# Pair 14's loads ahead of the output weights, a score bank for one turn, and one exponential behind a tanh

## The chip, the cores and the metric

The kernel runs on one core of one Trainium2 chip. The metric is device time in microseconds (us), the median of a few executions. One further execution was recorded by the hardware profiler; all times within the program are from it, in us from the start of its span.

## What is computed

Attention over 8 batches of 12 heads (448 rows, head size 64), with a softmax over the keys, and then a gated feed-forward block on the 3584 rows of 768 numbers that it gives. The reference, cut to what matters:

```python
scores = scale * np.matmul(q, k.transpose(0, 1, 3, 2))
attn = np.exp(scores - np.max(scores, axis=-1, keepdims=True))
attn = attn / (np.sum(attn, axis=-1, keepdims=True) + 1e-09)
x = np.matmul(attn, v)          # then heads are laid side by side: 3584 x 768
g = x @ w_gate                  # 768 x 1536
silu = g * (1.0 / (1.0 + np.exp(-g)))
out = (silu * (x @ w_val)) @ w_out   # w_out is 1536 x 768
```

## The kernel before

Two heads make a pair, so there are 48 pairs, six to a batch. The work on a pair has these steps, with the lines that the profile shows for them:

- **Loads.** GpSimd's DMA queue brings q, k and v from HBM and turns fp32 into fp16 on the way (`load_qk16`, L157 and, for keys of pairs from 12 on, L138 in two halves; `load_v`, L168 and L138). The same queue brings the weights: gate and value in quarters of two DMAs each (L186), the output weights in two halves, wo0 and wo1, of one DMA of 128 x 12 x 384 numbers each (L188). Pairs below 6 are loaded ahead of everything, some pairs two at a time. Pairs 14 and 15 share one buffer and are loaded apart.
- **Turning q and k.** For pairs up to 10 TensorE turns them (`prep`, L258) into a PSUM tile that VectorE copies out (L259). From pair 11 on GpSimd copies q and k into one fp16 tile (L217 for pair 11, `prep_quad` with L194 from 12 on), and SP issues two DMA transposes for each pair (L220 and L224, or L196 and L200). The copies stand in the same GpSimd stream as the DMA issues.
- **Scores and exponentials.** TensorE multiplies q and k into one of three score banks (L299; from pair 12 on L268, and L281 for a block of rows that two pairs share: that of 12 and 13 needs the turned q and k of both). ScalarE takes the exponential of each bank (L307, L289).
- **Product with v.** Lines L325 and L333, L362 from pair 12 on. VectorE divides by the sums (L344 and L346, or L403 and L404), and the result is turned into X (L433 on TensorE with L440 on VectorE for pairs below 12, DMA transposes on SP after that).
- **Feed-forward block.** Groups of six matmuls with gate and value weights (L493), a tanh on ScalarE (L511), two steps on VectorE (L516 forms t from the tanh and the gate product, L519 multiplies it with the value product), and twelve matmuls with the output weights for each part of the output (L544), which ScalarE copies out (L551) and SP stores (L564). The first block takes all its products with wo0 ahead of those with wo1.

PSUM has three score banks, taken in turn by `stile`, and two smaller buffers (tag `f`), which products of v, value products, output products and, in some visits, a gate product share.

The order is written out by hand. After an opening list, a plan runs through visits of two or three score products each (two below pair 8, three from there); in each visit come the scores and exponentials, then turns, loads and copies for later pairs, then the products with v that are due, and a share of the feed-forward work. A dictionary `wq` says which loads are issued at the end of the visit in which a pair's first score product stands: `6: [("V", 3), ("o", 0)]` brings v of pairs 9 to 11 and wo0, `9: [("o", 1)]` brings wo1. From pair 14 on, q and k of a pair are asked for six pairs ahead, that of 14 in the visit in which pair 8 begins. The copies of pair 11 stand in that visit too, those of 12 and 13 in the visit of pair 9, of 14 in that of pair 10, of 15 in that of pair 11.

A DMA that GpSimd issues waits, by the semaphores that the program uses in a ring of eight, until the eighth DMA before it has landed. The stream is in order, so what stands behind such a wait stands still as well.

Of the kernel before, what the change touches and what calls it, by code (L numbers as in the profile page):

```python
# [12 lines left out]
AF = mybir.ActivationFunctionType  # L13
# [7 lines left out]
LA = 6  # L21
RB = 5
FIRST = 6
# [8 lines left out]
QUAD = 12  # L32
# [5 lines left out]
def kernel(  # L38
# [10 lines left out]
    nc = tc.nc  # L49
    B, H, S, D = q.shape  # L50
    DM = H * D
    DF = moe_w_gate.shape[1]
    P = 112
# [4 lines left out]
    NPAIR = B * NHP  # L58
    NGRP = NPAIR // GP
    GPB = NHP // GP  # L60
    sm_scale = float(D) ** -0.5
# [41 lines left out]
    def wslice(kind, fb, cb):  # L103
        i, off = divmod(fb * 128, DF // 4)
        return wgv[kind, i][:, cb, ds(off, 128)]
# [9 lines left out]
    def stile():  # L115
        sring.append(sring.pop(0))
        return sbanks[sring[-1]]

    def dummy(n, w=512):
        wp = ps_f.tile([128, 512], FP32, tag="f", name="wp")  # L120
        for _ in range(n):
            nc.tensor.matmul(wp[:, 0:w], lhsT=warm[:, 0:128], rhs=warm[:, 0:w], start=True, stop=True)
# [39 lines left out]
    def load_v(pr, n=1):  # L162
        b, h = divmod(2 * pr, H)
        if pr >= QUAD:
            vd = vraw[:, ds(pr % VS, n)].rearrange("p r h c d -> p (r h) (c d)")
            load_keys(nc.gpsimd, vd, v, 2 * pr, 2 * n)
            return
        nc.gpsimd.dma_start(  # L168
            vraw[0:P, ds(pr % VS, n)].rearrange("p r h c d -> p (r h) (c d)"),
            v[b, h : h + 2 * n].rearrange("h (p c) d -> p h (c d)", c=NC),  # L170
        )
# [18 lines left out]
    def prep_quad(pr):  # L190
        rq, rk = raw[pr]
        qk16 = attp.tile([128, 2, NC, 2, D], FP16, tag="qk16", name="qk16", bufs=3)
        for dst, src in ((qk16[:, 0], rk), (qk16[0:P, 1], rq)):
            nc.gpsimd.tensor_copy(dst.rearrange("p c h d -> p h c d"), src)  # L194
        qkT[pr] = attp.tile([128, NC * 128 + S], FP16, tag="qkT", name="qkT", bufs=QB)
        nc.sync.dma_start_transpose(  # L196
            qkT[pr][:, 0 : NC * 128].rearrange("p (c q) -> p c q", q=128),
            qk16[:, 0].rearrange("p c h d -> p (c h d)"),
        )
        nc.sync.dma_start_transpose(  # L200
            qkT[pr][:, NC * 128 :].rearrange("p (c q) -> p c q", q=P),
            qk16[0:P, 1].rearrange("p c h d -> p (c h d)"),
        )

    def prep(pr):
        if pr >= QUAD:
            return prep_quad(pr)
        rq, rk = raw[pr]
        if pr == 0 or pr >= NPE:
            qk16 = attp.tile([128, 2, NC, 2, D], FP16, tag="qk16", name="qk16", bufs=3)[0:P]  # L210
            for t, src in enumerate((rq, rk)):
                dst = qk16[:, 1 - t].rearrange("p c h d -> p h c d")
                if pr == 0:
                    nc.vector.tensor_copy(dst[:, 0], src[:, 0])
                    nc.scalar.activation(dst[:, 1], src[:, 1], AF.Copy)
                else:
                    nc.gpsimd.tensor_copy(dst, src)  # L217
        qkT[pr] = attp.tile([128, 2 * S + D], FP16, tag="qkT", name="qkT", bufs=QB)
        if pr >= NPE:
            nc.sync.dma_start_transpose(  # L220
                qkT[pr][:, 0 : 2 * S].rearrange("p (c q) -> p c q", q=P),
                qk16.rearrange("p t c h d -> p (t c h d)"),
            )
            nc.sync.dma_start_transpose(  # L224
                qkT[pr][:, 2 * S :].rearrange("p (c q) -> p c q", c=1),
                qk16[0:D, 1, 0].rearrange("p h d -> p (h d)"),
            )
            return None

        def turn0():  # L230
            for t in range(2):
                tp = stile()
                for c in range(NC):
                    for hx in range(2):
                        nc.tensor.matmul(
                            tp[ts(hx, 64), c // 2, ds(c % 2 * P, P)],
                            lhsT=qk16[:, 1 - t, c, hx],
                            rhs=ident[0:P, 0:P],
                            start=True,
                            stop=True,  # L240
                        )
                dst = qkT[pr][:, ts(1 - t, S)].rearrange("p (a x) -> p a x", a=2)
                nc.vector.tensor_copy(dst[:, 0], tp[:, 0, 0 : 2 * P])
                nc.scalar.activation(dst[:, 1], tp[:, 1, 0 : 2 * P], AF.Copy)
                if t == 0:
                    dummy(1, 256)
                    nc.vector.tensor_copy(qkT[pr][:, 2 * S :], tp[:, 0, 0:D])

        def turn():
            if pr < FIRST + 2:  # L250
                tp = stile()[:, 0].bitcast(FP16)
            else:
                tp = ps_f.tile([128, 1024], FP16, tag="f", name="tp")
            for i in range(2 * NC + 1):
                t, c = (1 - i // NC, i % NC) if i < 2 * NC else (0, 0)
                for hx in range(2):
                    src = raw[pr][t][:, hx, c, :]
                    nc.tensor.transpose(tp[ts(hx, 64), ts(i, P)], src, ident[0:P, 0:P])  # L258
            nc.vector.tensor_copy(qkT[pr][:], tp[:, 0 : 2 * S + D])  # L259

        return turn if pr else turn0
# [28 lines left out]
            e[:, 0 : 2 * S].rearrange("p (h q) -> p h q", h=2), s[:, :, 0:S], AF.Exp, scale=sm_scale  # L290
        )

    def qk(pr, c):
        if pr >= QUAD:
            return qk_quad(pr, c)
        t = qkT[pr]
        s = stile()
        for hx in range(2):
            nc.tensor.matmul(  # L299
                s[:, hx, 0:S],  # L300
                lhsT=t[ts(hx, 64), c * P : c * P + 128],
                rhs=t[ts(hx, 64), ds(S + (1 - hx) * D, S)],
                start=True,
                stop=True,
            )
        e = Es[pr % NE][:, ds(c * EB, 16)].rearrange("p (h b) x -> p h (b x)", h=2)
        nc.scalar.activation(e[:, :, 0:S], s[0:P, :, 0:S], AF.Exp, scale=sm_scale)  # L307

    def qk_half(pr, half, between=None):
        for c in (2 * half, 2 * half + 1):  # L310
# [177 lines left out]
    def ffn1_steps(kk, c0, n, hts, ahead):  # L488
        for fb in range(NFB):

            def group(kind, dst):
                for cb in range(NCB):
                    nc.tensor.matmul(  # L493
                        dst[:, 0:n],
                        lhsT=wslice(kind, fb, cb),
                        rhs=X[kk][:, cb, ds(c0, n)],
                        start=(cb == 0),
                        stop=(cb == NCB - 1),
                    )

            if fb < ahead:
                gp, vp = sbanks[begun[fb]][:, 0], sbanks[begun[fb]][:, 1]
            elif gate_small[0]:
                gate_small[0] = False
                gp = ps_f.tile([128, 512], FP32, tag="f", name="gp")
            else:
                gp = stile()[:, 0]
            if fb >= ahead:
                group("g", gp)
            sg = fp.tile([128, 512], FP32, tag="sg")  # L510
            nc.scalar.activation(sg[:, 0:n], gp[:, 0:n], AF.Tanh, scale=0.5)  # L511
            if fb >= ahead:
                vp = ps_f.tile([128, 512], FP32, tag="f", name="vp")
                group("v", vp)
            t1 = fp.tile([128, 512], FP32, tag="t1")
            nc.vector.scalar_tensor_tensor(  # L516
                t1[:, 0:n], sg[:, 0:n], 1.0, gp[:, 0:n], ALU.add, ALU.mult
            )
            nc.vector.scalar_tensor_tensor(  # L519
                hts[:, fb, 0:n], t1[:, 0:n], 0.5 * HS, vp[:, 0:n], ALU.mult, ALU.mult  # L520
            )
            if fb < ahead:
                sring.append(begun[fb])
            yield
# [54 lines left out]
    with tc.manual_schedule():  # L579
# [5 lines left out]
        for vo in Vts:  # L585
# [18 lines left out]
            1: [("V", 2), ("qk", 8, 1), ("g", 1), ("v", 1)],  # L604
            3: [("qk", 9, 1), ("qk", 10), ("g", 2), ("v", 2)],
            4: [("g", 3), ("v", 3), ("qk", 12)],
            6: [("V", 3), ("o", 0)],
            9: [("o", 1)],
        }

        def emit(item):
# [9 lines left out]
        fvq = []  # L621
# [98 lines left out]
        while g < last or queue:  # L720
            n = 2 if g < WIDE * NC else 3
            todo = []
# [16 lines left out]
        for x, (chunks, todo) in enumerate(plan):  # L739
            quads = [u for u in chunks if u[0] >= QUAD and u[1] == RU]  # L740
            for pr, c in quads + [u for u in chunks if u not in quads]:
                if x > 0:
                    qk(pr, c)
            for _, p0 in todo:
                if p0 >= QUAD:
                    pv_piece(p0, RU)
# [7 lines left out]
            for pr in entered:  # L754
                lead = [pr + 3] if pr + 3 < QUAD else [pr + 3, pr + 4] if pr + 3 == QUAD else [pr + 4]
                for p in lead:
                    if NPE <= p < NPAIR:
                        prep(p)
                if 14 <= pr + LA < NPAIR:
                    load_qk16(pr + LA, 1)  # L760
                if 12 <= pr + 3 < NPAIR:
                    load_v(pr + 3)
# [86 lines left out]
```

## Time and profile before

| quantity | value |
|---|---|
| median of 3 executions | 453.12 us (452.09 to 453.83) |
| profiled execution, its own time | 452.5 us |
| its span, first to last instruction | 450.7 us |
| mean granted TensorE clock | 0.995 |
| TensorE busy | 438.9 us (97% of the span) |
| ScalarE, VectorE, GpSimd busy | 225.0, 199.9, 180.4 us |
| GpSimd's DMA queue (q0) | 24.56 MB, 48.7% of 16 DMA engines' span |
| DMA queue of SP (q1) | 24.66 MB, 28.7% |
| wo0 issued, landed | 46.9, 63.5 us |
| wo1 issued, landed | 64.8, 76.8 us |

Busy time is the sum of an engine's instructions. A wait is idle time of an engine, put down to the work that ended last before it went on. "DMA x from issue to landing" runs from the start of the issuing instruction until the completion is seen. In tables by stretches of time, the figure behind the busy times of the engines is the granted clock, then come the share of the DMA engines and GB/s.

### The profile page before, as it was taken

How to read it: one execution, taken by the hardware profiler on the slowest of the kernel's cores; microseconds unless marked ns; L12 is line 12 of the kernel's file. 1: busy time of each engine (PE TensorE's matmuls, PEld its weight loads, DVE VectorE, ACT ScalarE, POOL GpSimd, SP SyncE). 2: the span in 40 equal slices, each digit the busy share in tenths (PEclk: the TensorE clock that was granted, in tenths of full speed). 3: DMA queues.
4: the chain of work that ended last, by engine and by line, in shares of the span. 5: the costliest groups of instructions: out<-in, count | busy, mean ns of one | idle time of the engine just before them, and what ended most of it. 6: DMA issues, size and time to landing. Idle time of an engine off the chain costs nothing.

```text
span 450.7 us, 10033 instructions
## 1 busy us (share of the span) xinstructions
PE 438.9 (97%) x4025; PEld 246.7 (55%) x4025; DVE 199.9 (44%) x447; ACT 225.0 (50%) x332; POOL 180.4 (40%) x299
## 2 busy tenths in 40 slices
PE   8999998999999999999999999999999999999996
PEld 3665664544456566554556556554455656644464
DVE  4756551365564344343454434344444434045400
ACT  6975765546553654455536365455454651222222
POOL 8655735997875364336461366423000000000000
PEclk9999999899999999999999999999999999999999
DMA  9999999999997699975975688945131211200033
GB/s 140 176 200 201 197 172 174 154 201 160 134 142 94 108 140 120 125 119 69 125 109 101 111 128 106 155 78 97 32 79 47 50 43 23 79 27 0 0 107 105
DMA packets 108494, 49.90 MB, mean 111 GB/s; under 512 B 60832, under 2 KB 104992, under 8 KB 108448
## 3 DMA queue, kind: packets, MB, share of 16 engines
q0 software_dynamic: 46832, 24.56, 48.7%
q1 hardware_dynamic: 61520, 24.66, 28.7%
q8 instruction: 31, 0.51, 0.5%
q14 instruction: 15, 0.12, 0.1%
q10 hardware_dynamic: 96, 0.05, 0.0%
HBM read 49.55 MB, written 11.01 MB: 134 GB/s over the span
## 4 chain that ended last, share of the span: by engine, by line
PE 78%; DMA 14%; DVE 3%; POOL 2%; issue 1%; ACT 1%; DVEq 0%; ACTq 0%; POOLq 0%
PE op L544 23%; PE s L493 21%; PE vp L493 19%; PE acc L362 8%; DMA wv<-in_moe_w_val_dram 5%; PE s L268 4%; DMA k<-in_k_dram 3%; DMA wo<-in_moe_w_out_dram 3%; DMA wg<-in_moe_w_gate_dram 2%; DVE hts L519 1%; DVE t L516 1%; ACT sg L511 1%; PE s L281 1%; DMA vraw<-in_v_dram 1%; POOL k L157 1%
## 5 line engine op out<-in xcount | busy, mean ns | idle before, releaser
L493 PE MATMUL vp<-X,wv 128*128 128x512 f16 (+1 forms) x564 | 122.4, 353 | 0.1
L544 PE MATMUL op<-wo,hts 128*128 128x384 f16 (+1 forms) x684 | 116.6, 325 | 2.6 <-DMA wo<-in_moe_w_out_dram 2.2
L493 PE MATMUL s<-X,wg 128*128 128x512 f16 (+1 forms) x534 | 116.4, 354 | 0.0
L289 ACT ACTIVATE E<-s 128x896 f16<-128x896 f32 x126 | 106.5, 921 | 13.6 <-PE s L268 8.7
L516 DVE SCALAR_TENSOR_TENSOR t<-sg,s 128x512 f32<-128x512 f32 (+1 forms) x91 | 56.7, 623 | 107.3 <-ACT sg L511 107.3
L511 ACT ACTIVATE sg<-s 128x512 f32<-128x512 f32 (+1 forms) x91 | 49.9, 549 | 93.6 <-PE s L493 91.1
L544 PEld LDWEIGHTS <-hts 128*128 128x128 f16 x684 | 66.1, 98 | 48.3 <-issue 2.9
L493 PEld LDWEIGHTS <-wv 128*128 128x128 f16 x564 | 55.1, 98 | 52.1 <-issue 0.4
L551 ACT ACTIVATE osb<-op 128x384 f32<-128x384 f32 (+1 forms) x57 | 27.7, 486 | 103.7 <-PE op L544 102.3
L493 PEld LDWEIGHTS <-wg 128*128 128x128 f16 x564 | 52.4, 98 | 44.9 <-issue 0.7
L519 DVE SCALAR_TENSOR_TENSOR hts<-t,vp 128x512 f16<-128x512 f32 (+1 forms) x94 | 58.5, 622 | 10.2 <-DVE t L516 0.5
L194 POOL COPY qk<-k 128x512 f16<-128x512 f16 x36 | 22.8, 632 | 99.3 <-DMA qkT<-qk 97.5
L138 POOL DMA_DIRECT2D vraw<-in_v_dram x72 | 43.8, 627 | 9.8 <-DMA wo<-in_moe_w_out_dram 6.5
L138 POOL DMA_DIRECT2D k<-in_k_dram x70 | 42.3, 616 | 7.0 <-DMA wo<-in_moe_w_out_dram 4.8
L362 PEld LDWEIGHTS <-E 128*128 128x128 f16 (+1 forms) x1152 | 37.2, 96 | 13.1 <-issue 7.6
L307 ACT ACTIVATE E<-s 112x896 f16<-112x896 f32 x48 | 40.7, 917 | 6.6 <-PE s L299 5.8
L403 DVE RECIPROCAL R<-acc 128x4 f32<-128x4 f32 x68 | 12.0, 177 | 70.9 <-PE acc L362 70.9
L362 PE MATMUL acc<-vo,E 128*128 128x65 f16 (+1 forms) x1088 | 40.8, 193 | 2.2 <-DVE hts L519 1.9
L157 POOL DMA_DIRECT2D q<-in_q_dram x44 | 30.1, 683 | 5.3 <-PE acc L333 1.8
L404 DVE TENSOR_TENSOR xt<-acc,R 128x256 f16<-128x256 f32 x68 | 28.8, 424 | 2.3
L268 PE MATMUL s<-qkT 64*128 64x448 f16 x216 | 28.3, 355 | 0.0
L194 POOL COPY qk<-q 112x512 f16<-112x512 f16 x36 | 23.1, 642 | 0.0
(70 smaller groups left out, 208.6 us busy)
## 6 DMA issues: line engine op xcount, KB each, us to landing
vraw<-in_v_dram POOLq DMA_DIRECT2D x72, 64.0 KB, 4.5
q<-in_q_dram POOLq DMA_DIRECT2D x41, 112.0 KB, 3.8
k<-in_k_dram POOLq DMA_DIRECT2D x68, 64.0 KB, 4.5
wg<-in_moe_w_gate_dram POOLq DMA_DIRECT2D x8, 288.0 KB, 9.8
wv<-in_moe_w_val_dram POOLq DMA_DIRECT2D x8, 288.0 KB, 10.2
wo<-in_moe_w_out_dram POOLq DMA_DIRECT2D x2, 1152.0 KB, 14.3
out_dram<-osb SPq DMA_DIRECT2D x8, 288.0 KB, 3.7
out_dram<-osb SPq DMA_DIRECT2D x6, 336.0 KB, 2.8
```

Source lines behind the costliest of these rows:

```text
L138: eng.dma_start(dst[ts(s, 64)], rows)
L157: nc.gpsimd.dma_start(dst[0:P, ds(h0, 2 * n)], flat.rearrange("h (p c) d -> p h (c d)", c=NC))
L194: nc.gpsimd.tensor_copy(dst.rearrange("p c h d -> p h c d"), src)
L268: nc.tensor.matmul(s[:, hx, 0:S], lhsT=t[ts(hx, 64), ts(c + low(pr, hx), 128)], rhs=t[ts(hx, 64), ds(NC * 128, S)], start=True, stop=True,)
L289: nc.scalar.activation(e[:, 0 : 2 * S].rearrange("p (h q) -> p h q", h=2), s[:, :, 0:S], AF.Exp, scale=sm_scale)
L307: nc.scalar.activation(e[:, :, 0:S], s[0:P, :, 0:S], AF.Exp, scale=sm_scale)
L362: nc.tensor.matmul(accs[pr][0][hx][:, ts(j, D + 1)], lhsT=e[rows, ds(hx * S + j * 128, 128)], rhs=Vts[pr % NV][rows, hx, col, 0 : D + 1], ...
L493: nc.tensor.matmul(dst[:, 0:n], lhsT=wslice(kind, fb, cb), rhs=X[kk][:, cb, ds(c0, n)], start=(cb == 0), stop=(cb == NCB - 1),)
L511: nc.scalar.activation(sg[:, 0:n], gp[:, 0:n], AF.Tanh, scale=0.5)
L516: nc.vector.scalar_tensor_tensor(t1[:, 0:n], sg[:, 0:n], 1.0, gp[:, 0:n], ALU.add, ALU.mult)
L519: nc.vector.scalar_tensor_tensor(hts[:, fb, 0:n], t1[:, 0:n], 0.5 * HS, vp[:, 0:n], ALU.mult, ALU.mult)
L544: nc.tensor.matmul(op[:, 0:w], lhsT=hts[:, fb, ts(ch, 128)], rhs=wo[oh][:, fb, ds(m0 - oh * OH, w)], start=(fb == 0), stop=(fb == NFB - 1),)
```

## The change

Three edits in the order of work. First, q and k of pair 14 are asked for in the visit of pair 6, behind v of 9 to 11 and ahead of wo0, and wo1 follows in the visit of pair 7; the loads from pair 15 on stay six pairs ahead. In GpSimd's stream that makes wo0 and wo1 neighbours, with the copies of pairs 11 to 13 behind both. Second, pair 8 is turned in a score bank and not in a buffer of tag `f`; the score banks that the visits after it use move on by one. Third, where a visit has three score products, no product with v and feed-forward steps left, the last exponential is issued behind the visit's first tanh. In the order of instructions this holds in one visit, that with the last product of pair 8 and the first two of pair 9.

```diff
         def turn():
-            if pr < FIRST + 2:
+            if pr < FIRST + 3:
                 tp = stile()[:, 0].bitcast(FP16)
...
-    def qk(pr, c):
+    exps_behind = []
+
+    def qk(pr, c, behind=False):
...
-        nc.scalar.activation(e[:, :, 0:S], s[0:P, :, 0:S], AF.Exp, scale=sm_scale)
+
+        def exp():
+            nc.scalar.activation(e[:, :, 0:S], s[0:P, :, 0:S], AF.Exp, scale=sm_scale)
+
+        if behind:
+            exps_behind.append(exp)
+        else:
+            exp()
...
             nc.scalar.activation(sg[:, 0:n], gp[:, 0:n], AF.Tanh, scale=0.5)
+            while exps_behind:
+                exps_behind.pop(0)()
...
-            6: [("V", 3), ("o", 0)],
-            9: [("o", 1)],
+            6: [("V", 3), ("qk", 14, 1), ("o", 0)],
+            7: [("o", 1)],
...
-                    qk(pr, c)
+                    qk(pr, c, not todo and len(chunks) == 3 and (pr, c) == chunks[-1] and pr < QUAD and bool(fvq))
...
-                if 14 <= pr + LA < NPAIR:
+                if 15 <= pr + LA < NPAIR:
                     load_qk16(pr + LA, 1)
```

## The prediction, made before the result

> **What bounds the kernel now.** I read the page first, then TensorE's waits, the chain, and last the timelines of TensorE, GpSimd and the DMA queues in the stage that the chain pointed to.
>
> ```profile
> PE 438.9 (97%) x4025; PEld 246.7 (55%) x4025; DVE 199.9 (44%) x447; ACT 225.0 (50%) x332; POOL 180.4 (40%) x299
> L544 PE MATMUL op<-wo,hts 128*128 128x384 f16 (+1 forms) x684 | 116.6, 325 | 2.6 <-DMA wo<-in_moe_w_out_dram 2.2
> ```
>
> TensorE is busy in 97% of the span, and the change leaves its instructions and their order as they are. Only its waits, and a slow clock, can be won. All waits of TensorE that the change can touch are these:
>
> ```profile
> PE op L544 <- DMA wo<-in_moe_w_out_dram: 2.2, 1, 2.2
> PE tp L258 <- DVE t L516: 0.7, 1, 0.7
> PE acc L325 <- DVE t L516: 0.4, 1, 0.4
> ```
>
> The second half of the output weights (wo1) is late once; two PSUM buffers come free late. The chain shows why wo1 is late:
>
> ```profile
> 45.69 1.23 issue
> 47.96 1.17 POOL qk L217 x2
> 50.38 14.42 DMA k<-in_k_dram
> 64.79 12.04 DMA wo<-in_moe_w_out_dram
> 76.88 3.16 PE op L544 x12
> ```
>
> The keys of pair 14, asked for at 50.38, lie behind wo0 in GpSimd's queue and land at 64.8; only then is wo1 asked for, and it lands at 76.8. Here twelve products took 3.16 us; in the timeline below a like group takes 2.12. The table by microseconds says why:
>
> ```profile
> 78.00:79.00 1.00, 1.00 (x5) 0.49 (x4) 0.00 (x0) 0.00 (x0) 0.69 (x2) 0.50 1.38 183
> 79.00:80.00 1.00, 1.00 (x6) 0.49 (x5) 0.00 (x0) 0.00 (x0) 1.00 (x2) 0.50 1.35 185
> ```
>
> The granted clock (third figure from the right) is 0.50; over the microseconds from 77 to 82 it reads 0.90, 0.50, 0.50, 0.50, 0.89, so 0.10 + 3 x 0.50 + 0.11 = 1.71 us of clock are lost after the 2.22 us wait. The late wo1 costs 3.9 us in all.
>
> Who needs what, on TensorE, and what GpSimd does before it:
>
> ```profile
> 64.06 0.74 PE L299 MATMUL s<-qkT 64*128 64x448 f16 x6
> 65.82 4.07 PE L544 MATMUL op<-wo,hts 128*128 128x384 f16 x24
> 69.99 0.36 PE L299 MATMUL s<-qkT 64*128 64x448 f16 x2
> 70.66 2.12 PE L544 MATMUL op<-wo,hts 128*128 128x384 f16 x12
> 72.72 0.38 PE L281 MATMUL s<-qkT 64*64 64x448 f16 x4
> ```
>
> ```profile
> 46.92 1.04 POOL L188 DMA_DIRECT2D wo<-in_moe_w_out_dram  x1 [1.33 <-issue]
> 47.96 0.62 POOL L217 COPY qk<-q 112x512 f16<-112x512 f16 x1
> 48.51 0.62 POOL L217 COPY qk<-k 112x512 f16<-112x512 f16 x1
> 64.79 1.03 POOL L188 DMA_DIRECT2D wo<-in_moe_w_out_dram  x1 [0.35 <-DMA k<-in_k_dram]
> ```
>
> The reader is to see that pair 11's copies (L217) follow wo0 at once; after the change wo1 stands between them. The scores of pair 11 start at 64.06 and need its turned q and k; the scores of 12 follow at 69.99, the joint row block of 12 and 13 (L281) at 72.72. Their transposes landed at 59.6, 65.2 and 69.5, slack of 4.5, 4.8 and 3.2 us.
>
> ```profile
> q0 software_dynamic: 186, 0.14, 90.7%
> q1 hardware_dynamic: 189, 0.05, 36.4%
> ```
>
> Packets from 57 to 58 us: with weights (q0) and transposes (q1) both pending, each queue moves the same number. Beside q, k and v packets it is 257 each (64 to 65); wo alone moves about 260 a microsecond, q, k and v alone about 390 (51 to 52).
>
> [...]
>
> **The change part by part.** (1) The loads. On GpSimd the order becomes: v of 9 to 11, q14, k14 (two DMAs), wo0, wo1, copies of 11, 12, 13, then q15 and the rest. Nothing is added; three issues (0.67 + 1.24 us) move ahead of wo0, and one (1.03 us) ahead of the copies. SP's order is unchanged, but its transposes follow the copies. Every GpSimd DMA waits for the eighth DMA before it, so wo1 waits for q12, issued at 40.42 and landed 10.9 us later, at 51.3. Room is the second bound: wo0 stood until 2,190 packets were outstanding (issued, by the shapes: 112 x 2 for a pair's q, 64 x 2 for each half of k, 128 x 12 for wo; less those that q0 had moved by then); after the change about 2,780 are outstanding at 51.3, and at 390 a microsecond the same room is there at 52.8. So wo1 is issued between 51.3 and 52.8, ends 1.05 later, and the copies of 11 (1.2 us) end between 53.5 and 55.1, not at 49.1. The copies of 12 had waited for k12, landed at 52.7; they now end 1 to 2.5 us later.
>
> wo0: 480 data packets of pair 14 go ahead of it and cost 1.3 us, but the transposes start later and leave it the queue alone. By packets it ends at about 60.5 and lands between 62.7 and 64.4 (before: 63.5). It is needed at 65.8; no wait. wo1 follows it with 1,536 packets at 186: 8.3 us, landed by 71 to 72.8, 2 us ahead of 74.66 where it was missed. The 2.22 + 1.7 = **3.9 us go**.
>
> Transposes: from issue to first packet took 4.0 us at 49.16 and 4.2 at 66.47. Pair 11 then starts between 57.5 and 59.2, moves 960 packets (8 x 112 + 64) at 186 (5.2 us) and lands 1.3 later: **64.0 to 65.7**, up to 66.4 if the 0.7 us in which both queues stood still near 60.6 come again. TensorE asks at 64.06 or a little earlier, so it waits 0 to 3 us. Pair 12 lands at about 69.6 to 71.5. Pair 13 follows, partly beside q, k and v packets at 257 (3.8 to 5.2 us, 2.3 to landing), and lands at **75 to 77**; it is wanted at 72.72. TensorE then stands 2.3 to 4.3 us later than before at that row; I take 3.5. This is the larger of the waits and not their sum: what it lost at pair 11 it need not wait for again. Pair 14 lands by 80, wanted at 78.5 + 3.5; pair 15 by 82, wanted at 85 + 3.5. GpSimd now stops at k16 until wo1 has landed at 71 to 73; behind it are v13 and the copies of 15 (done by 75) and nobody else.
>
> Whether a new wait halves the clock again is unknown: 0.7 us did not, 2.2 us did. Price 0 to 1.7 us. At pair 11 it costs nothing more, since 13 is later still; it counts only if the wait at pair 13 is the long one. I take 0.
>
> (2) Pair 8's turn in a score bank: the 18 transposes at 34.35 waited 0.68 us for a buffer held by L516. The bank's last reader, L519, ends at 33.84, so 0.47 can go; the next scores take the neighbouring banks, whose exponentials end at 35.3, which gives part back. Bound -0.47 to +0.3; I take -0.2.
>
> (3) The exponential: the order on ScalarE differs in one place, the last one of the visit at 51.39, now behind the tanh of 53.80. The tanh starts about 0.7 earlier, L516 too, and the 0.36 us wait at 54.95 goes; but the bank of the third score comes free at 54.5 and not 53.9. Bound -0.36 to +0.3; I take -0.1. TensorE arrives earlier at 64.06 through (2) and (3) and only waits longer for pair 11, whose loads run on the DMA queue's time: in the sum they count nothing while that wait stands. If the cover goes, they are worth 0.3.
>
> Sum: -3.9 + 3.5 = **-0.4 us**. The profiled execution took 452.5 (span 450.7 and 1.8 around it), 0.6 below the median of 453.12. From the execution that is 452.1, from the median 452.7; I give 452.7.
>
> **The rivals.** *The transposes land in time* (chance 0.27): if there is room for wo1 at 51.3, and packets run as smoothly as from 62 to 65, pair 11 waits under 1 us and 13 about 1.5, so -2.4, to -4.7 with (2) and (3) whole: 448.4 to 450.8. For it: the room is inferred from one wait. Against: slack at pair 13 was only 3.2 us. *The wait for pair 13 halves the clock* (0.28), the other side: it lands at 77 or later, TensorE reaches L281 early enough to wait over 2 us, [...]: 4.5 + 1.7 - 3.9 = +2.3 and more, 455.4 to 457. It decides from a landing of about 76.9. For it: the same happened at wo1; against: a wait at pair 11 would shorten this one. *The change does nothing*: wo1 is in fact issued where it stood; the instruction order excludes it. The forecast (waits traded within 2.2 us) has 0.45.
>
> **How the numbers follow.** About 0.5% (2.3 us) is what a measurement of this kernel can tell from no change. The forecast's own range is 451 to 455, all within it; the first rival gives faster 0.27, the second slower 0.28, and same 0.45. The range for 8 in 10 goes into both rivals: 449.3 to 456.2.
>
> **What would show it.** Right: no wait of op L544 for wo; a wait of s L299 for qkT near 64 and of L281 near 73; wo1 issued at 52 to 53; pair 11's copies ending past 53.5. Wrong: op L544 waiting for wo0 at 65.8; wo1 issued past 54; scores of 11 to 13 without a wait; or differences after 95 us, where the orders are the same.

## The result, and the profile after

The changed kernel takes 453.77 us (median of 6 runs, 452.63 to 454.64); the kernel before, run beside it, takes 452.94 us (6 runs, 452.09 to 454.26). The ratio is 1.0014 with a 95% interval of 0.9992 to 1.0037: no difference that can be measured. Ratios are taken over all runs here, so they need not be the quotient of the two medians. The profiled executions, one of each kernel, stand the same way, 453.37 us (span 451.6) after and 452.5 (span 450.7) before. Line numbers have moved with the edits: L299, L307, L325, L346, L404, L440, L466, L493, L519, L544 of before are L301, L311, L334, L355, L413, L449, L475, L502, L530, L555 after; those up to L281 are the same. The loads alone and the kernel with only wo1 moved keep the numbers of before.

TensorE's work has not changed, and the wait for wo1 has gone. From the page of the changed kernel, its engines and the group of the output products:

```profile
PE 439.0 (97%) x4025; PEld 247.1 (55%) x4025; DVE 201.7 (45%) x447; ACT 224.8 (50%) x332; POOL 180.3 (40%) x299
L555 PE MATMUL op<-wo,hts 128*128 128x384 f16 (+1 forms) x684 | 116.4, 325 | 0.4 <-DVE xt L413 0.4
```

The idle time ahead of the output products was 2.6 us and is 0.4. It has moved to the scores. TensorE's waits after (us in total, times, longest), those that the change touched:

```profile
PE s L301 <- DMA qkT<-qk: 2.7, 1, 2.7
PE s L281 <- DMA qkT<-qk: 0.6, 1, 0.6
...
PE s L301 <- ACT E L311: 0.3, 1, 0.3
PE s L268 <- DVE X L475: 0.3, 1, 0.3
...
PE s L258 <- DVE hts L530: 0.2, 1, 0.2
```

The transposes of pair 11 (L301) are now late by more than wo1 was before, and those of pair 13 (L281) are late once more. The last line is the turn of pair 8 in its score bank: 0.2 us where a buffer of tag `f` had cost 0.7; the third line is what it gives back. The 0.4 us wait of a product with v behind the exponential is gone.

The chain of waits after leads over other transfers than before. These are its longest pieces between 38 and 80 us (start, duration, what):

```profile
38.34 12.39 DMA wv<-in_moe_w_val_dram
50.74 1.30 issue
52.04 1.33 POOL wo L188 x2
56.85 20.38 DMA qkT<-qk x2
79.20 1.95 PE op L555 x12
```

The keys of pair 14 and wo have given their places to the transposes. GpSimd's timeline shows what made these late (start, duration, line, count, and in brackets the idle time before):

```profile
49.07 0.59 POOL L138 DMA_DIRECT2D k<-in_k_dram  x1 [0.91 <-DMA wv<-in_moe_w_val_dram]
52.04 2.05 POOL L188 DMA_DIRECT2D wo<-in_moe_w_out_dram  x2 [2.38 <-issue]
54.08 0.63 POOL L217 COPY qk<-q 112x512 f16<-112x512 f16 x1
54.63 0.63 POOL L217 COPY qk<-k 112x512 f16<-112x512 f16 x1
```

After k14 GpSimd stands still for 2.38 us, then issues both halves of wo, and only at 54.1 does it reach the copies of pair 11, which had started at 47.96 before. On TensorE that becomes:

```profile
66.16 0.74 PE L301 MATMUL s<-qkT 64*128 64x448 f16 x6 [2.75 <-DMA qkT<-qk]
...
76.32 0.37 PE L281 MATMUL s<-qkT 64*64 64x448 f16 x1
77.27 0.38 PE L281 MATMUL s<-qkT 64*64 64x448 f16 x3 [0.58 <-DMA qkT<-qk]
...
82.44 0.36 PE L268 MATMUL s<-qkT 64*128 64x448 f16 x2 [0.32 <-DVE X L475]
...
88.14 0.38 PE L281 MATMUL s<-qkT 64*64 64x448 f16 x4
```

Pair 11's scores start at 66.16 (before 64.06), the rest of the joint row block at 77.27 (before 72.72), and the last line, which in the kernel before starts at 87.25, lies 0.89 us later, which is the whole difference of these two spans. The clock was halved here too. From the table by microseconds of the changed kernel (granted clock third from the right):

```profile
67.00:68.00 1.00, 1.00 (x23) 1.00 (x21) 0.00 (x0) 1.00 (x2) 1.00 (x3) 0.50 1.29 192
68.00:69.00 1.00, 1.00 (x15) 0.79 (x13) 0.23 (x2) 1.00 (x2) 0.54 (x1) 0.50 1.28 190
```

From 66 to 71 us it reads 0.98, 0.50, 0.50, 0.50, 0.81: 0.02 + 1.50 + 0.19 = 1.71 us of clock lost, as much as behind the late wo1.

### The profile page after: what moved, and what is told of

Its sections match the earlier page's. It is cut to its first block, busy times and chain, and to the rows that moved or that the text cites. A ratio compares the mean times of both kernels' runs of the same rounds, so it can differ in the third digit from the quotient of the medians.

```text
span 451.6 us, 10034 instructions
## 1 busy us (share of the span) xinstructions
PE 439.0 (97%) x4025; PEld 247.1 (55%) x4025; DVE 201.7 (45%) x447; ACT 224.8 (50%) x332; POOL 180.3 (40%) x299
## 3 DMA queue, kind: packets, MB, share of 16 engines
q0 software_dynamic: 46832, 24.56, 47.2%
## 4 chain that ended last, share of the span: by engine, by line
PE 77%; DMA 12%; POOL 4%; DVE 3%; issue 2%; ACT 1%; SPq 0%; DVEq 0%; ACTq 0%; POOLq 0%
PE op L555 23%; PE s L502 21%; PE vp L502 19%; PE acc L371 8%; DMA qkT<-qk 5%; PE s L268 4%; DMA wv<-in_moe_w_val_dram 3%; DMA vraw<-in_v_dram 3%; DMA k<-in_k_dram 2%; DVE hts L530 1%; DVE t L527 1%; PE s L281 1%; ACT sg L520 1%; POOL q L157 1%; POOL k L157 1%
## 5 line engine op out<-in xcount | busy, mean ns | idle before, releaser
L502 PE MATMUL vp<-X,wv 128*128 128x512 f16 (+1 forms) x564 | 122.4, 353 | 0.1
L555 PE MATMUL op<-wo,hts 128*128 128x384 f16 (+1 forms) x684 | 116.4, 325 | 0.4 <-DVE xt L413 0.4
L502 PE MATMUL s<-X,wg 128*128 128x512 f16 (+1 forms) x534 | 116.4, 354 | 0.0
L555 PEld LDWEIGHTS <-hts 128*128 128x128 f16 x684 | 66.2, 98 | 46.1 <-issue 3.2
L502 PEld LDWEIGHTS <-wv 128*128 128x128 f16 x564 | 55.1, 98 | 52.1 <-issue 0.4
L502 PEld LDWEIGHTS <-wg 128*128 128x128 f16 x564 | 52.3, 98 | 44.9 <-issue 0.7
L530 DVE SCALAR_TENSOR_TENSOR hts<-t,vp 128x512 f16<-128x512 f32 (+1 forms) x94 | 58.5, 622 | 10.1 <-DVE t L527 0.5
L311 ACT ACTIVATE E<-s 112x896 f16<-112x896 f32 x48 | 40.5, 916 | 8.7 <-PE s L301 8.5
L413 DVE TENSOR_TENSOR xt<-acc,R 128x256 f16<-128x256 f32 x68 | 28.9, 425 | 2.3
L268 PE MATMUL s<-qkT 64*128 64x448 f16 x216 | 28.1, 353 | 0.3 <-DVE X L475 0.3
```

What stands on the lines that cost most here:

```text
L268: nc.tensor.matmul(s[:, hx, 0:S], lhsT=t[ts(hx, 64), ts(c + low(pr, hx), 128)], rhs=t[ts(hx, 64), ds(NC * 128, S)], start=True, stop=True,)
L502: nc.tensor.matmul(dst[:, 0:n], lhsT=wslice(kind, fb, cb), rhs=X[kk][:, cb, ds(c0, n)], start=(cb == 0), stop=(cb == NCB - 1),)
L530: nc.vector.scalar_tensor_tensor(hts[:, fb, 0:n], t1[:, 0:n], 0.5 * HS, vp[:, 0:n], ALU.mult, ALU.mult)
L555: nc.tensor.matmul(op[:, 0:w], lhsT=hts[:, fb, ts(ch, 128)], rhs=wo[oh][:, fb, ds(m0 - oh * OH, w)], start=(fb == 0), stop=(fb == NFB - 1),)
```

## The experiments

**What was to be told apart.** The theory: the change trades waits, because in GpSimd's stream the copies of pairs 11 to 13 stand behind wo1, and the transposes come late by about what wo1 was late. A second account put the missing gain down to the edits on TensorE's side, the turn and the exponential. A third held that GpSimd's DMA queue is full in any case, so that whatever order is taken, something is late by the same amount. If the first is right, an order that keeps the copies ahead of wo1 and still asks for wo1 early must be faster by about 3 us; if the third is right, it must not. Every kernel ran beside the kernel before, and the time given for that one was measured at the same time.

### The loads alone

```diff
 before
-            6: [("V", 3), ("o", 0)],
-            9: [("o", 1)],
+            6: [("V", 3), ("qk", 14, 1), ("o", 0)],
+            7: [("o", 1)],
...
-                if 14 <= pr + LA < NPAIR:
+                if 15 <= pr + LA < NPAIR:
```

> Only the loads are moved (pair 14 ahead of wo0, wo1 in the visit of pair 7); pair 8's turn and the exponential stay as before. Theory A (the copies of pairs 11 to 13 stand behind both halves of wo in GpSimd's stream, so their transposes land late and set TensorE's time): as the whole change, 453.8 us within 0.6, with a wait of the L299 scores for qkT of 2 to 3 us at about 63.5 and one at L281. Rival B (the turn in a score bank or the moved exponential cost what the loads win): 2 to 4 us faster than before, 449 to 451, without a wait for qkT over 1 us.

453.41 us (22 runs) beside 453.5 (42 runs), ratio 1.0011 (0.9998 to 1.0025). TensorE's waits in this kernel:

```profile
PE s L299 <- DMA qkT<-qk: 2.1, 1, 2.1
...
PE tp L258 <- DVE t L516: 0.7, 1, 0.7
PE s L281 <- DMA qkT<-qk: 0.5, 1, 0.5
...
PE acc L325 <- DVE t L516: 0.4, 1, 0.4
```

The loads alone do what the whole change does. The two waits that the turn and the exponential take away are still here (0.7 and 0.4), and the wait at pair 11 is shorter by 0.7 (2.06 rather than 2.75): TensorE comes later, and pair 11's scores start at nearly the same time (66.03 and 66.16).

### The turn and the exponential alone

The changed kernel with the three lines above put back.

> Only the turn of pair 8 and the exponential are moved; the loads stay as before. Theory A: TensorE gains 0.3 to 0.5 us by 55 us, and gives it back where it waits for wo1, which lands on the DMA queue's time: the wait for wo grows from 2.2 to about 2.6 us and the total is that of before within 0.4 us (452.9). Rival B: the two edits cost time of their own, 1 us or more. Rival C: their gain of 0.5 us stays in the total (452.4).

453.54 us (14 runs) beside 453.5, ratio 1.001 (0.9993 to 1.0026). The wait:

```profile
PE op L555 <- DMA wo<-in_moe_w_out_dram: 3.2, 1, 3.2
```

What the two edits gain can be read off TensorE's timelines: from its gate product at 31 us to its turn of X at 63 us, just ahead of pair 11's scores, it takes 32.7 to 32.9 us in the four traces without the two edits and 32.3 in eight with them, so about 0.4 us are left of the 0.7 + 0.4. Here they end at wo1, which lands on its own time. The wait was longer than the 2.6 us expected, 0.3 us of it because in this execution TensorE went on with wo1 at 77.18 rather than at 76.88; and behind it the clock was low (0.50) for twice as long as before, for a loss of 3.41 us. Each part of the change alone is worth nothing, then, for the same reason: behind it stands a transfer that doesn't come sooner.

### The copies of pair 11 ahead of the output weights

```diff
 after
-            6: [("V", 3), ("qk", 14, 1), ("o", 0)],
-            7: [("o", 1)],
+            6: [("V", 3), ("qk", 14, 1)],
+            8: [("o", 0), ("o", 1)],
```

> The changed kernel, with both halves of wo issued in the visit of pair 8, behind the copies of pair 11 and ahead of those of 12 and 13; the order within the DMA queue stays that of the changed kernel. Theory A: the copies of 11 end at about 51, no wait of L299 for qkT; pair 13 lands 2 to 4 us earlier than in the changed kernel (about 72 to 74), so at most 1 us of wait is left at L281; wo0 lands at 64 to 65 and is hardly missed: 449 to 451. Rival D (what delays the transposes is that wo0 and wo1 lie in the queue together, by packets, and not the order of GpSimd's stream): pair 13 still lands at 75 or later, 452.5 to 454.

450.38 us (13 runs) beside 453.5, ratio 0.9938 (0.9922 to 0.9955). GpSimd in this kernel:

```profile
49.18 0.62 POOL L217 COPY qk<-q 112x512 f16<-112x512 f16 x1
49.73 0.62 POOL L217 COPY qk<-k 112x512 f16<-112x512 f16 x1
51.50 2.15 POOL L188 DMA_DIRECT2D wo<-in_moe_w_out_dram  x2 [1.15 <-issue]
```

The same DMAs stand in the same order; only the two copies of pair 11 (1.2 us of work) have gone ahead of wo. No scores wait for pair 11, the mean granted clock of the profiled execution is 0.999, and both halves of wo arrive in time though they are issued at much the same moment as after the change. What is left is 0.94 us at L268 for VectorE and 0.36 at L281 for a later pair. This is the test between the first and the third account: the queue was not too full, the copies were too late.

### Only wo1 earlier, behind k14

The loads as before, with wo1 in the visit of pair 8, where k14 and the copies of pair 11 stand ahead of it. With the turn and the exponential of the change, measured three times:

```diff
 after
-            6: [("V", 3), ("qk", 14, 1), ("o", 0)],
-            7: [("o", 1)],
+            6: [("V", 3), ("o", 0)],
+            8: [("o", 1)],
...
-                if 15 <= pr + LA < NPAIR:
+                if 14 <= pr + LA < NPAIR:
```

> Turn and exponential as changed; loads as before, but wo1 issued in the visit of pair 8, right behind pair 14 and ahead of the copies of pairs 12 and 13 (before: in the visit of pair 9). Theory A: wo0 and the copies of 11 keep their times of before; wo1 is issued at 51.3 to 52.5, waits for the DMA of q12, costs the copies of 12 nothing since they wait for k12 until 52.7, and lands at 73 to 74.5: no wait for wo over 0.5 us and none for qkT over 0.5 us, 448.5 to 450. Rival D: transposes and wo1 slow each other by packets, so that wo1 lands at 75 to 76 or pair 13 is late: 450.5 to 453.

> The same kernel as e4, timed beside its variants: 0.7% faster than before again.

> The same kernel as e4, beside its variant: 0.7 to 0.9% faster than before again.

| run | us (6 runs each) | before | ratio, 95% interval | longest wait at L268 |
|---|---|---|---|---|
| first | 449.82 | 453.5 | 0.9932 (0.9908 to 0.9956) | 1.40 us |
| again | 449.22 | 453.39 | 0.9911 (0.9889 to 0.9934) | 1.09 us |
| third | 450.37 | 453.22 | 0.9933 (0.9915 to 0.9951) | 1.77 us |

Faster than both kernels in all three: no wait for wo and none for pair 11 is left. What is left is a wait for VectorE at L268. In the third run, VectorE:

```profile
76.49 1.02 DVE L175 COPY vo<-vraw 128x512 f16<-128x512 f16 x1 [1.77 <-DMA vraw<-in_v_dram]
77.43 0.55 DVE L449 CAST X<-xtp 128x384 f16<-128x384 f32 x1
77.90 0.54 DVE L475 CAST X<-s 128x384 f16<-128x384 f32 x1
```

The copy of v of pair 12 (L175) stands ahead of the two casts that free the banks; v is asked for behind wo1 and lands late, and VectorE stands 1.77 us for it. It is the pattern of this case once more, on another engine: an instruction that waits for a DMA, with work behind it that somebody needs.

### v of pair 12 ahead of wo1

```diff
 the kernel with wo1 behind k14
-            8: [("o", 1)],
+            8: [("V1", 12), ("o", 1)],
...
+            elif item[0] == "V1":
+                load_v(item[1])
...
-                if 12 <= pr + 3 < NPAIR:
+                if 13 <= pr + 3 < NPAIR:
                     load_v(pr + 3)
```

> As the kernel with wo1 behind pair 14 (e4), and v of pair 12 issued ahead of wo1. In e4 VectorE stood from 75.1 to 77.06 for v of pair 12, which lies behind wo1 in the queue, and TensorE waited 1.40 us for the copy L475 behind it on VectorE. Theory A: that wait goes (under 0.3 us), wo1 is issued about 1.3 us later (53 to 54) and still lands ahead of 75, so 1.0 to 1.4 us less than e4. Rival D: wo1 or pair 13, now about 1 us later in the queue, is late by as much, and the total is that of e4 within 0.4 us.

450.29 us (6 runs) beside 449.22 for the kernel that it was to better; ratio to before 0.9934 (0.9912 to 0.9955). The wait at L268 went down to 0.3, and others came:

```profile
PE s L281 <- DMA qkT<-qk: 1.7, 2, 1.0
...
PE op L555 <- DMA wo<-in_moe_w_out_dram: 0.9, 1, 0.9
```

In this trace the third account holds, on a smaller scale: with v ahead, wo1 and the transposes of pairs 13 and 15 are late, by 2.6 us in sum against about 1 us saved. The profiled execution was the slowest of the six (451.44 us), and the intervals of the two kernels touch: the 1.0 to 1.4 us that v ahead was to bring are ruled out, but that it costs time is not shown.

### The copy of v behind the casts

The kernel with wo1 behind k14, and VectorE's copy of v of pair 12 issued behind the casts L449 and L475 rather than ahead of them; no DMA moves.

```diff
+            late = [p0 for p0 in vcopies.get(x, []) if p0 not in early]
+            behind = XPE - 1 in [p0 for _, p0 in todo]
-            for p0 in vcopies.get(x, []):
-                if p0 not in early:
+            for p0 in late:
+                if not behind:
                     copy_v(p0)
...
+            for p0 in late:
+                if behind:
+                    copy_v(p0)
```

> As e4 (wo1 behind pair 14), and VectorE's copy of v of pair 12 put behind the two copies into X (L449, L475) of the same visit; loads as in e4. Theory A: the 1.1 to 1.4 us wait of TensorE at L268 for L475 shrinks to 0.3 us, the products with v of pair 12 wait at most 0.3 us for the copy: 0.8 to 1.1 us less than e4 in the same call. Rival: v of pair 12 lands so late (76.8) that the products with v wait for the copy instead, and the total is that of e4 within 0.4 us.

449.73 us (6 runs) beside 450.37 for the third run above and 453.22 for before; ratio to before 0.9922 (0.99 to 0.9944). VectorE in this kernel:

```profile
77.09 0.56 DVE L449 CAST X<-xtp 128x384 f16<-128x384 f32 x1 [1.25 <-PE xtp L442]
77.56 0.55 DVE L475 CAST X<-s 128x384 f16<-128x384 f32 x1
78.03 0.33 DVE L175 COPY vo<-vraw 128x512 f16<-128x512 f16 x1
```

The casts wait for TensorE alone, the wait at L268 is 0.32 us, and no wait of TensorE for this stage is above 0.4. The step of 0.6 us is in the direction of the trace but short of the 0.8 to 1.1 expected, and the intervals of the two kernels overlap, so the gain is not shown.

### Only wo1 earlier, without the turn and the exponential

```diff
 before
-            9: [("o", 1)],
+            8: [("o", 1)],
```

> Before, with wo1 issued in the visit of pair 8 and nothing else: turn and exponential as before. Theory A: with no wait on the DMA queue left ahead of 75 us to swallow it, the gain of the turn and the exponential (0.5 us by the traces) now counts, unless TensorE only waits longer for VectorE's copy of v of pair 12, whose data lands on the queue's time: the total is that of e4 within 0.3 us, with a wait at L268 of about 1 us instead of 1.4. Rival C: 0.5 us slower than e4.

450.55 us (11 runs) beside 449.22 with the two edits, measured at the same time, and 453.39 for before; ratio to before 0.9943 (0.9924 to 0.9961). The difference of 1.3 us is outside the 0.3 expected. Since the kernel with the two edits itself lies between 449.22 and 450.37 in its three measurements, the runs leave their worth between about 0.2 and 1.3 us, and the intervals overlap. The traces show 0.4 us by 63 us, and behind it a wait for VectorE at L268 (1.3 us here), where the kernel with the two edits waits behind v of pair 12. One line of the plan brings most of what can be had here.

### The output weights in smaller DMAs

Each half of wo as two DMAs of 128 x 6 x 384 numbers; everything else as before.

```diff
 before
-            dst = wo[i]
+            for t in range(2):
+                nc.gpsimd.dma_start(wo[i][:, ts(t, NFB // 2)], src[:, ts(t, NFB // 2)])
+            return
```

> Before, with each half of wo issued as two DMAs of 128 x 6 x 384. One look, for the 1.2 to 1.3 us of 'issue' ahead of wo0. If it is room for 1536 packets, the first part (768) is issued without it and the second stands. If it belongs to the first issue of wo as such, the first part shows about 1.2 us and the second none. If it is neither, both show under 0.4 us.

449.81 us in one run beside 453.39. Its GpSimd:

```profile
46.30 0.83 POOL L181 DMA_DIRECT2D wo<-in_moe_w_out_dram  x1 [0.40 <-DMA wg<-in_moe_w_gate_dram]
48.71 0.83 POOL L181 DMA_DIRECT2D wo<-in_moe_w_out_dram  x1 [1.58 <-issue]
```

The first half of wo0 goes out at 46.30 with hardly a wait; the stand that wo0 had in the kernel before (1.33 us of "issue") is now ahead of the second. TensorE's wait for wo is 1.2 us rather than 2.2, and the clock is not halved (mean 1.0). These come to 1.0 + 1.7 us; where the rest of the 3.6 us comes from is open, and one run doesn't settle the size.

### wo0 ahead of v

```diff
 the kernel with wo1 behind k14
-            6: [("V", 3), ("o", 0)],
+            6: [("o", 0), ("V", 3)],
```

> As e4, with wo0 ahead of v of pairs 9 to 11 in GpSimd's stream. One look, for the 1.3 us of 'issue' that stood ahead of wo0 in every kernel and, in the split one, ahead of its second part. [...] If it belongs to wo0 (its size, or the first DMA of this kind), it stays ahead of wo0.

457.54 us in one run beside 453.22: a wrong move, and a useful one.

```profile
PE vp L502 <- DVE xt L355: 6.9, 1, 6.9
```

v of pairs 9 to 11 lies behind wo0 in the queue, VectorE waits for it, and TensorE waits 6.9 us for VectorE. On GpSimd wo0 went out at 45.19 after 0.92 us for earlier weights, and the DMA of v behind it stood for 1.63 us. The timeline puts this down to VectorE's L355, which ended at 47.80; but in the kernel before the same DMA went out at 44.82, ahead of that instruction (L346 there, 47.26), so it can't have needed it.

## Why the prediction was right

It said 452.7 us with "within 0.5%" as the likeliest, and the time is 453.77 (ratio 1.0014): the waits were traded. The mechanism that it gave is the one in the traces, though one reason in it failed and two terms of its sum were off. Step by step:

- **The late wo1 goes.** Forecast: landed by 71 to 72.8, no wait, 3.9 us gained. It landed at 71.8, and the wait and its halved clock are gone. wo0, forecast at 62.7 to 64.4 without a wait, landed at 63.6 without one.
- **The copies of pair 11.** Forecast to end between 53.5 and 55.1; they ended at 55.3, and wo1 went out at 53.06 (forecast 51.3 to 52.8, with 54 as the point where the forecast fails). Right in size.
- **Why they are late: this reason failed.** The prediction bounded wo1's issue by "room", that is, wo0 had stood until 2,190 packets were outstanding: the author's estimate from one wait, since no view shows a limit of the queue. Worked out in the same way, only some 720 were outstanding when wo0 went out after the change, and yet it stood 1.30 us longer than the landing it waited for; wo1 followed at once. In the second run of the kernel with wo1 behind k14, wo1 went out with about 2,670 outstanding and no such stand. A count of outstanding packets does not explain it. That the forecast of 52.8 came so close is luck in part. The prediction's other bound, the eighth DMA before wo1 (q of pair 12), is a wait that the timelines show: GpSimd stood for 6.47 us until wo0 had landed before it issued the eighth DMA behind it (63.84, kernel before), and for 3.54 us until wo1 had landed before the eighth behind that (72.08, after). For wo1 its end was put at 51.3, and q landed at 52.4 (issued at 40.57, 11.8 us to landing), so without the stand wo1 could have gone out only about 0.7 us sooner: the wrong term cost little.
- **The transposes.** Four microseconds from issue to the first packet (55.28 to about 59), then equal counts of packets with the weights: the tables of the DMA queues show 190 and 194 (61 to 62 us), 187 and 186 (66 to 67). Before the change they had shown 186 and 189 (57 to 58), and on these the forecast rested. Pair 11 was forecast to land at 64.0 to 65.7, up to 66.4, and landed at 66.05; pair 12 at 69.6 to 71.5, and landed at 71.8; pair 13 at 75 to 77, and landed at 77.2. All at the late end or just past it.
- **The slack.** The prediction put the landings before the change at 59.6, 65.2 and 69.5. Those of pairs 11 and 13 were misread: the last transpose of 11, issued at 50.56, took 8.6 us and that of 13, issued at 58.16, took 10.5, so they landed at 59.2 and 68.7. The slack was 4.9, 4.8 and 4.1 us rather than 4.5, 4.8 and 3.2. The sum doesn't use these figures, and pair 13 still has the least.
- **The waits on TensorE.** At pair 11 0 to 3 us were forecast, 2.75 came. At pair 13 TensorE was to be later than before by 2.3 to 4.3 us, taken at 3.5: it was later by 77.27 - 72.72 = 4.55. This is the term that was too small, by 1.05, because the landing was taken near the middle of its bounds.
- **The clock.** It was halved (0.50), at pair 11. The prediction took 0 for it and said why it costs nothing there: "13 is later still". So it was. Even with 1.71 us of clock lost TensorE came to L281 at 76.32, ahead of the transposes, and waited 0.58. Without the loss it would have waited there for 2.3. That is one execution. The 22 of the loads alone fall into two groups, 13 from 452.75 to 453.83 (among them the profiled one, and five with a mean clock of 1.000) and nine from 454.50 to 455.44, none of these at full clock; the medians are 1.9 us apart. A halved clock that counts in some executions, at pair 13 for example, would look like this. No trace of a slow one was kept, so this is not shown.
- **The turn and the exponential.** Taken at -0.2 and -0.1 and counted as nothing while the wait for pair 11 stands. The loads alone and the two edits alone bear that out: neither moves the time. On TensorE's timelines the turn brings 0.15 us (from 31 to 37 us, 5.71 before and 5.56 after) and the exponential 0.25 (from 52 to 60 us, 8.01 and 7.76), so the sizes were nearly right. What they are worth in the total with the cover gone, put at 0.3, the runs leave between 0.2 and 1.3.
- **The sum.** -3.9 + 4.55 = 0.65. The remaining 0.24 of the 0.89 us at 88.14 belongs mostly to the 0.32 us wait for L475 at 82.44, which the kernel before doesn't show, probably because its clock was still halved until 81.21, so that TensorE came no sooner than VectorE.

Of the rivals, the one of transposes in time failed at pair 13, which had 4.1 us of slack and landed 8.6 us later. The one of a halved clock at pair 13 didn't come about in the profiled execution because the wait at pair 11 had taken its share first, as the prediction held against it; its condition, a landing at about 76.9 or later, was met. What it counted for the clock is the 1.7 us lost behind the late wo1 before.

The time that the change was to win does exist. With the copies ahead of wo it is 3.1 us below the kernel before (450.38), with wo1 moved behind k14 2.9 to 4.2 us, and 2.8 where that one line is all that is changed.

## What to carry to other kernels

In a stream that runs in order and holds both DMA issues and work that others wait for, an issue is priced by what stands behind it: ask of every transfer that is moved ahead which small step it passes, and who needs that step next. Two copies of 0.6 us each, put behind weights that nobody needed yet, cost the whole gain. And when a stall goes, list the slack of the next consumers (here 4.9, 4.8 and 4.1 us) beside the delay that the move gives them (6.9, 6.5 and 8.6 us); the largest excess of delay over slack sets the new end.

## What the runs showed of the hardware

**In three traces the clock fell for 3.41 us, in a fourth for twice as long.** Tables of the granted clock by tenths of a microsecond place its fall and its return: 77.80 and 81.21 in the kernel before, 66.97 and 70.38 after, 79.23 and 82.64 in the third run of the kernel with wo1 behind k14, 75.75 and 82.58 with the turn and the exponential alone. The first three stretches have 3.41 us, the last twice that; the clock in them is 0.50. The kernel before stood for 2.22 us and lost 1.71 of clock; the third run stood for only 1.77 and lost as much. The table of the third run:

```profile
79.00:80.00 1.00, 1.00 (x24) 1.00 (x24) 0.40 (x2) 0.81 (x1) 1.00 (x3) 0.61 0.79 80
80.00:81.00 1.00, 0.92 (x7) 0.42 (x5) 0.95 (x4) 0.00 (x0) 1.00 (x3) 0.50 1.40 201
81.00:82.00 1.00, 1.00 (x5) 0.47 (x4) 0.10 (x1) 0.00 (x0) 1.00 (x2) 0.50 1.28 150
82.00:83.00 1.00, 1.00 (x6) 0.49 (x4) 0.00 (x0) 0.00 (x0) 1.00 (x3) 0.68 1.09 157
```

The wait of 1.77 us ended at 78.49, and the clock fell 0.7 us later, in the middle of full work. In the 3.41 us ahead of the four falls TensorE was idle for 2.22, 2.61, 1.77 and 1.81 us. Behind the last of them it was idle for another 1.43 us, and there the clock stayed low for 6.83; a wait of 1.40 us in the first run of the kernel with wo1 behind k14, whose mean clock was 1.0, halved nothing. Where the limit lies, and what sets the moment of the fall, was not measured, since no run varied a wait by itself. For the kernel it means that a wait of about 2 us (1.77 and 2.22 here) can cost another 1.7.

The spread of the kernel before agrees. Of the 42 executions beside the first experiments, six had a mean clock of 1.000 and a median of 451.56 us, 26 had 0.995 or 0.996 and 453.28, and ten had 0.991 or 0.992 and 454.24. One stretch, 1.71 us lost in 452, lowers the mean by 0.004, so by this estimate these had none, one and two stretches. The same program may thus pay for its wait with none, one or two of them; only the profiled executions show where the stretches lie.

**A DMA of GpSimd stood about 1.2 to 1.6 us at one place in the count of packets.** The packets of GpSimd's DMAs are added up from the start (rows, and 16 more for each DMA, which gives the queue's total of 46,832 in the kernel before). There are four different orders, and the DMA that stands is wo0 before (15,408 to 16,960), wo0 after (15,936 to 17,488), the second part of the split wo0 (16,192 to 16,976), and with wo0 ahead of v the DMA of v (16,272 to 16,960), while wo0 (14,720 to 16,272) goes through. What these have in common is the stretch from 16,272 to 16,960, and each of 11 traces has the stand on a DMA that covers it. Stands of up to 1.63 us put down to issue lie elsewhere too (at 292.08 us after the change). The agreement is all that was found; what makes the DMA stand was not tried.
